# Decode bits on ScalarE, part of x on TensorE, and whole output rows in a fused attention and mixture-of-experts kernel

## The chip, the cores and the metric

The kernel runs on 1 core of one Trainium2 chip. A core has TensorE (matmuls and the loads of their weights, PE and PEld in the tables), VectorE (DVE), ScalarE (ACT), GpSimd (POOL), SyncE (SP, which here issues the DMAs), and 16 DMA engines. Each engine works through its own list of instructions in order. The metric is device time in microseconds. The kernel before takes 516.57 us, the median of 3 runs (515.62 to 517.06).

## The reference, cut to what matters

Three layers follow each other on 3072 tokens. In the first, a recurrence with decay is written here as one step per token; the kernel does it in blocks of 128 tokens.

```python
def _attn_ref(r, k, v, w, u):             # (4, 8, 768, 48) each, fp32
    state = np.zeros((B, H, D, D)); y = np.zeros_like(r)
    for t in range(S):
        cur = np.einsum('bhd,bhe->bhde', u[None] * kt, vt)
        y[:, :, t] = np.einsum('bhd,bhde->bhe', rt, state + cur)
        state = wt[:, :, :, None] * state + np.einsum('bhd,bhe->bhde', kt, vt)
    return y

def _moe_ref(x, w_in, w_out):             # x (3072, 384); weights Float64
    h = x @ w_in                          # (3072, 2048)
    return ((h * np.cos(h)) @ w_out).astype(np.float32)

def _moe2_ref(x, phi, w1, w2):            # soft routing over 32 slots, 8 experts
    logits = x @ phi
    d = softmax over tokens of logits;  slot_input = d.T @ x
    slot_out[e] = np.maximum(slot_input[e] @ w1[e], 0.0) @ w2[e]
    c = softmax over slots of logits
    return c @ slot_out                   # (3072, 384) fp32
```

## The kernel before

**Tiling.** The 3072 tokens are 24 blocks j of 128. For each block the attention part makes transposes, two scans (L150, L158), small matmuls (A, U, y) and at last `x`, the block's output with channels on the partitions. x is kept as two parts, a rounded one and a remainder. ScalarE copies the high part out of PSUM with rounding (`xh`, L289), VectorE subtracts it from the PSUM tile to get the low part (`xl`, L293). The matmuls of the second layer (`h`, L413 to L415) take three products of such parts: nine matmuls of 512 columns for one bank, four banks per block. Each bank passes through `turns` (ScalarE, L428), `rest` (VectorE, L432), `cos` (ScalarE, L436), `mul` (VectorE, L440) and transposes (`gT`, L447), and is reduced to slot logits (`l`, L462) and slot sums (`E`, L558).

**Decoding the weights.** `w_in` and `w_out` come as Float64. They are read as pairs of 32-bit words in 16 pieces of 768 numbers per partition, eight of each matrix (`raw`, L308 and L314), and turned into fp32 by bit operations, four steps a piece. `abs` on ScalarE (L319) takes the high word, scaled so that its bits stand nearly in place; `d1` on VectorE (L323) shifts them left by three; `d2a` on VectorE (L328) puts the sign in; `d2b` on VectorE (L334) shifts the low word right by 29 and sets these three bits. A piece of `w_in` is then also split: `whi` (ScalarE, L344) rounds it, `wn` on TensorE (L355, L356) makes the piece minus its rounded part by two products with the identity and with `neg`, its negative, and `wc` (ScalarE, L361) copies the remainder. Pieces of `w_out` are transposed (L367), copied (L373) and multiplied with `phi`.

**Order.** All this is one long table of steps, HEAD. Its order is the order of the instructions on every engine; nothing is reordered afterwards. A step's name and numbers call one of the functions below: `d1.i.3` is `e_shift("i", 3)`, `xl.0` is `e_xl(0)`. The first DMAs are the constants `cs` (L599), then pieces 0 and 1 of `w_in`.

**End.** After the 24 blocks come the 8 experts (L746, L786) and the output. The output is c @ slot_out for 24 tiles of 128 tokens. Its 384 columns are made in two parts, 256 and 128 wide, since the second part of `slot_out` (`so`, and rounded as `sr`) is ready later. `outputs(i, n0)` makes part i for two or four tiles at a time: matmuls (L817 for the first four tiles, L819 for the others), one copy of the PSUM bank by ScalarE or VectorE (L826), one DMA (L827). Its rows are 1 KB long in part 0 and 512 bytes in part 1.

Of the kernel before, what the change touches and what calls it, by code (L numbers as in the profile page):

```python
# [21 lines left out]
def rwkv_moe_kernel(ctx: ExitStack, tc: tile.TileContext, r, k, v, w, u, w_in, w_out, phi, w1, w2, cst, out):  # L22
# [21 lines left out]
    JA = 6  # L44
    ATT = 77
# [22 lines left out]
    dec = d_stack.enter_context(tc.tile_pool(name="dec", bufs=4))  # L68
# [230 lines left out]

    def e_raw(x, n):  # L300

        if x == "i":
# [295 lines left out]
    if True:  # L598
        nc.sync.dma_start(cs, cst)  # L599
# [3 lines left out]
        nc.scalar.mul(neg, ident, -1.0)  # L603
# [43 lines left out]
        def exp_table():  # L647
            nc.scalar.activation(half_pi[:, 1:2], half_pi[:, 0:1], AF.Exp)

        step = {"tab": exp_table, "quart": lambda g: s_quarters(g, lcp[g]), "esl": lambda g, hf: s_e(g, slice(hf * 256, hf * 256 + 256)),  # L650
                "misc": misc, "raw": e_raw, "abs": e_abs, "d1": e_shift, "d2a": e_sign, "d2b": e_d2b, "whi": e_whi, "wlo": e_wlo, "oT": e_oT, "oc": e_oc, "om": e_om,
# [56 lines left out]
        with tc.manual_schedule(engines=ORDERED):  # L708
# [92 lines left out]
            obs = {}  # L801

            def outputs(i, n0, tile_=None):
# [23 lines left out]
                nc.sync.dma_start(out[(n0 * nt + t0) * 128:(n0 * nt + t1) * 128, cols].rearrange("(t p) f -> p t f", p=128), ob)  # L827

# [167 lines left out]
```

## Time and profile before

| | |
|---|---|
| median of 3 runs | 516.57 us (515.62 to 517.06) |
| the profiled execution | 517.23 us |
| its span in the trace | 515.5 us |
| busy in the span | TensorE 475.0, VectorE 426.2, ScalarE 318.6, GpSimd 103.1 us |
| the chain that ended last, by engine | TensorE 70%, VectorE 20%, ScalarE 4%, issue 3% |
| mean granted clock of TensorE | 0.986 of 2.4 GHz |

The span is what the trace covers, from the first to the last event; 1.73 us of the execution lie outside it. Busy time of TensorE is modelled, since its matmuls are pipelined. Which engine limits the kernel differs from stage to stage, so the table's shares are averages over stages; a view of busy time in separate stretches tells more.

### The profile page before, as it was taken

How to read it: one execution, taken by the hardware profiler on the slowest of the kernel's cores; microseconds unless marked ns; L12 is line 12 of the kernel's file. 1: busy time of each engine (PE TensorE's matmuls, PEld its weight loads, DVE VectorE, ACT ScalarE, POOL GpSimd, SP SyncE). 2: the span in 40 equal slices, each digit the busy share in tenths (PEclk: the TensorE clock that was granted, in tenths of full speed). 3: DMA queues.
4: the chain of work that ended last, by engine and by line, in shares of the span. 5: the costliest groups of instructions: out<-in, count | busy, mean ns of one | idle time of the engine just before them, and what ended most of it. 6: DMA issues, size and time to landing. Idle time of an engine off the chain costs nothing.

```text
span 515.5 us, 15594 instructions
## 1 busy us (share of the span) xinstructions
PE 475.0 (92%) x6515; PEld 369.7 (72%) x6515; DVE 426.2 (83%) x842; ACT 318.6 (62%) x702; POOL 103.1 (20%) x127
## 2 busy tenths in 40 slices
PE   1778899999999999999999999999999989997994
PEld 1545578887877787778878778778787777864573
DVE  2999999999997989979998899998898975664423
ACT  3476678776576566666756767757566655573421
POOL 2133231122423221132212312241211000002200
PEclk9979999999999999999999999999999999999997
DMA  9998384932540930505532208224311964089948
GB/s 263 268 267 152 117 207 112 173 70 53 94 78 3 145 57 3 93 3 82 91 62 40 42 17 136 50 49 80 65 19 28 409 263 156 17 309 355 399 142 269
DMA packets 144758, 67.47 MB, mean 131 GB/s; under 512 B 127153, under 2 KB 133553, under 8 KB 144689
## 3 DMA queue, kind: packets, MB, share of 16 engines
q1 hardware_dynamic: 144688, 66.49, 51.2%
q8 instruction: 51, 0.84, 0.7%
q14 instruction: 19, 0.15, 0.1%
HBM read 61.75 MB, written 4.72 MB: 129 GB/s over the span
## 4 chain that ended last, share of the span: by engine, by line
PE 70%; DVE 20%; ACT 4%; issue 3%; DMA 1%; SPq 0%; DVEq 0%; ACTq 0%
PE h L413 11%; PE h L415 10%; PE h L414 10%; PE gT L447 7%; PE l L462 4%; PE y L275 4%; PE E L558 3%; PE A L196 2%; PE hps L746 2%; PE so L786 2%; DVE lt L179 2%; PE U L247 2%; DVE pt L158 2%; PE kT L135 2%; DVE qt L150 2%
## 5 line engine op out<-in xcount | busy, mean ns | idle before, releaser
L413 PE MATMUL h<-wu,x 128*128 128x512 f32 x288 | 119.3, 414 | 1.1 <-DVE g L440 0.6
L415 PE MATMUL h<-wu,x 128*128 128x512 f32 x288 | 113.0, 392 | 0.0
L414 PE MATMUL h<-wu,x 128*128 128x512 f32 x288 | 112.4, 390 | 0.0
L436 ACT ACTIVATE g<-g,half_pi 128x512 f32<-128x512 f32 x97 | 69.0, 718 | 28.5 <-DVE g L432 27.6
L428 ACT ACTIVATE g<-h 128x512 int32<-128x512 f32 (+1 forms) x96 | 57.1, 597 | 47.5 <-PE h L415 43.5
L440 DVE TENSOR_TENSOR g<-g,h 128x512 f32<-128x512 f32 x96 | 64.9, 677 | 12.4 <-ACT g L436 11.4
L432 DVE SCALAR_TENSOR_TENSOR g<-g,h 128x512 f32<-128x512 int32 (+1 forms) x96 | 64.5, 677 | 10.8 <-ACT g L428 9.7
L210 POOL TENSOR_SCALAR_AFFINE_SELECT lt<-bo 64x512 f32<-64x512 f32 x48 | 38.1, 794 | 173.8 <-ACT bo L238 89.5
L413 PEld LDWEIGHTS h<-wu,x 128*128 128x128 f32 x288 | 54.2, 188 | 15.6 <-DVE g L440 4.3
L453 ACT COPY gt<-gT 128x512 f32<-128x512 f32 x89 | 51.8, 583 | 19.9 <-PE gT L447 15.1
L415 PEld LDWEIGHTS h<-wu,x 128*128 128x128 f32 x288 | 54.0, 188 | 12.0
L414 PEld LDWEIGHTS h<-wu,x 128*128 128x128 f32 x288 | 54.3, 189 | 9.2
L447 PE MATMUL gT<-cs,g 128*128 128x128 f32 x384 | 58.6, 278 | 0.8 <-DVE g L440 0.5
L447 PEld LDWEIGHTS gT<-cs,g 128*128 128x128 f32 x384 | 43.5, 141 | 11.9 <-issue 2.0
L163 POOL TENSOR_TENSOR ru<-rn,u_b 128x384 f32<-128x384 f32 x24 | 27.7, 1154 | 116.7 <-DVE bo L233 57.5
L222 DVE COPY_PREDICATED lt<-cs,A 64x256 f32<-64x256 uint32 x72 | 32.2, 447 | 3.0 <-PE A L196 1.4
L261 ACT COPY rzs<-z 64x192 f32<-64x192 f32 x96 | 33.4, 348 | 2.0 <-DVE z L256 1.0
L179 DVE TENSOR_TENSOR lt<-rT,pt 64x512 f32<-64x512 f32 x48 | 32.8, 684 | 0.8 <-PE y L275 0.3
L462 PE MATMUL l<-gt,p_sb 128*32 128x128 f32 x768 | 32.1, 277 | 0.3 <-DVE gt L453 0.3
L158 DVE TENSOR_TENSOR_SCAN pt<-wf,ini_f 128x520 f32<-128x520 f32 x24 | 30.7, 1278 | 0.2
L150 DVE TENSOR_TENSOR_SCAN qt<-wf,one_b 128x520 f32<-128x520 f32 x24 | 29.7, 1236 | 0.1
L275 PE MATMUL y<-lt,rzs 128*32 128x64 f32 x1536 | 26.6, 220 | 3.2 <-issue 3.2
(165 smaller groups left out, 769.0 us busy)
## 6 DMA issues: line engine op xcount, KB each, us to landing
we<-in_moe_w_dram SPq DMA_DIRECT2D x16, 1536.0 KB, 9.3
rawo<-in_moe_w_out_dram SPq DMA_DIRECT2D x8, 768.0 KB, 5.1
wn<-in_w_dram SPq DMA_DIRECT2D x24, 192.0 KB, 4.1
kn<-in_k_dram SPq DMA_DIRECT2D x24, 192.0 KB, 4.4
rawi<-in_moe_w_in_dram SPq DMA_DIRECT2D x3, 1536.0 KB, 10.2
rn<-in_r_dram SPq DMA_DIRECT2D x24, 192.0 KB, 3.4
vn<-in_v_dram SPq DMA_DIRECT2D x24, 192.0 KB, 3.7
rzs<-in_v_dram SPq DMA_DIRECT2D x96, 48.0 KB, 3.0
```

Of the source, the lines that this page charges most:

```text
L179: nc.vector.tensor_tensor(out=L[h, a], in0=ps[h], in1=segs(pt, 0, C)[h], op=ALU.mult)
L275: nc.tensor.matmul(ps[m:m + 32, o, c * C:(c + 1) * C], lhsT=rz[:, c, p, a, 32 * b:32 * b + 32], rhs=L[:, a, 2 * p + c, :], start=m not in ...
L413: nc.tensor.matmul(half[:, f], lhsT=xh[:, c, :], rhs=wh, start=(c == 0), stop=False)
L414: nc.tensor.matmul(half[:, f], lhsT=xl[:, c, :], rhs=wh, start=False, stop=False)
L415: nc.tensor.matmul(half[:, f], lhsT=xh[:, c, :], rhs=wl, start=False, stop=(c == KD - 1))
L428: nc.scalar.activation(gt.bitcast(I32), hp, AF.Copy, bias=0.25, scale=1.0 / TWO_PI)
L432: nc.vector.scalar_tensor_tensor(out=gt, in0=gt.bitcast(I32), scalar=-TWO_PI, in1=hp, op0=ALU.mult, op1=ALU.add)
L436: nc.scalar.activation(gt, gt, AF.Sin, bias=half_pi[:, 0:1])
L440: nc.vector.tensor_tensor(out=gt, in0=gt, in1=hp, op=ALU.mult)
L447: nc.tensor.transpose(ps[:, m * 128:(m + 1) * 128], gt[:, m * 128:(m + 1) * 128], ident)
L453: (nc.vector.tensor_copy if n >= ATT and n % 8 in (1, 2, 5) else nc.scalar.copy)(gt_t[t, q], pend.pop(("gT", t, q)))
L462: nc.tensor.matmul(lps_t[g][32 * m:32 * m + 32, o:o + TB], lhsT=p_sb[:, 4 * q + m, :], rhs=gt[:, m * 128:(m + 1) * 128], start=first, stop ...
```

## The change

Four things change, and the whole table HEAD is written in another order.

1. **Decode.** A step `q` (`e_low`) on ScalarE takes the low word, as an unsigned integer, to the three bits that it gives: it scales by about 2^-29, adds a bias and writes an integer. `d2a` now puts the sign into that integer tile, and `d2b` shifts the high part by three and joins the two in one VectorE instruction. `d1` is gone. All 16 pieces are in the set LOW. A piece of `w_out` is decoded in place in `wo_sb`, so the pool `dec` holds two tiles of each kind instead of four.
2. **Low part of x.** For blocks 0 to 5 `xl` is replaced by `xm` on TensorE, which adds the negative of the high part to the PSUM tile, and `xc` on ScalarE, which copies the tile out with rounding. Blocks 6 to 23 keep `xl`.
3. **Start.** Piece 1 of `w_in` is the first DMA, ahead of `cs` and piece 0. Pieces 2 and 3 come as two DMAs, not one.
4. **Output.** Tiles 0 to 9 are made as before. Tiles 10 to 23 are made by `rows(k)` when both parts of `sr` are there: two matmuls of 384 columns, whose weights are every other token of 256, two copies, one by each engine, and one DMA in which every partition holds two whole rows, 3072 bytes.

```diff
-    dec = d_stack.enter_context(tc.tile_pool(name="dec", bufs=4))
+    dec = d_stack.enter_context(tc.tile_pool(name="dec", bufs=2))
...
-    neg = sm_p.tile([128, G], F32R, tag="lg", name="neg", bufs=1)[:, 0:128]
+    neg = nat.tile([128, 128], F32R, name="neg")
...
+    def e_xm(j):
+        nc.tensor.matmul(pend["xT", j], lhsT=neg, rhs=xo(j)[0], start=False, stop=True, skip_group_check=True)
+
+    def e_xc(j):
+        nc.scalar.copy(xo(j)[1], pend.pop(("xT", j)))
...
     def e_abs(x, n):
-        a_t[x, n] = dec.tile([128, 768], F32, tag="a", name=f"a{x}{n}")
+        a_t[x, n] = dec.tile([128, 768], F32, tag="a", name=f"a{x}{n}") if x == "i" else wo_sb[:, 2 * n:2 * n + 2, :].rearrange("p m n -> p (m n)")
...
+    def e_low(x, n):
+        q_i[x, n] = dec.tile([128, 768], I32, tag="q", name=f"q{x}{n}", bufs=2)
+        nc.scalar.activation(q_i[x, n].rearrange("p (k f) -> p k f", k=KD), raw_t[x, n][..., 0].bitcast(U32), AF.Copy,
+                             bias=7.5 * 2.0 ** -17 - 0.5, scale=2.0 ** -29 * (1.0 - 2.0 ** -17))
...
-        hi, ai = raw_t[x, n][..., 1], a_t[x, n].bitcast(I32).rearrange("p (k f) -> p k f", k=KD)
+        hi, ai = raw_t[x, n][..., 1], (q_i[x, n] if (x, n) in LOW else a_t[x, n].bitcast(I32)).rearrange("p (k f) -> p k f", k=KD)
...
+        if (x, n) in LOW:
+            nc.vector.scalar_tensor_tensor(out=ai, in0=ai, scalar=3, in1=q_i[x, n], op0=ALU.logical_shift_left, op1=ALU.bitwise_or)
+            return
...
-        nc.sync.dma_start(cs, cst)
...
+            NA = 10
...
+            crf = cr.rearrange("p j b t -> p (j b t)")
+
+            def rows(k):
+
+                m = k - NA // 2
+                if m in (0, 4):
+                    obs["r"] = wu_p.tile([128, 4, 2, DM], F32, tag=f"wu{1 if m == 0 else 2}", name=f"obr{m}")
+                ob = obs["r"][:, m % 4]
+                for i in range(2):
+                    ps = pb(f"r{k}_{i}")[:, 0:DM]
+                    nc.tensor.matmul(ps, lhsT=crf[:, 256 * k + i:256 * k + 256:2], rhs=sr, start=True, stop=True)
+                    (nc.vector.tensor_copy if i else nc.scalar.copy)(ob[:, i], ps)
+                nc.sync.dma_start(out[256 * k:256 * k + 256, :].rearrange("(p i) f -> p (i f)", i=2), ob.rearrange("p i f -> p (i f)"))
...
             nc.vector.tensor_copy(so[:, parts[1]], ops[1][:, 0:128])
-            for n0 in range(9, 12):
-                outputs(0, n0)
+            outputs(1, 0)
             slots_out(1)
             slots_round(1)
-            for n0 in range(6):
+            for n0 in range(1, (NA + 3) // 4):
                 outputs(1, n0)
+            for k in range(NA // 2, NTT // 2):
+                rows(k)
...
-raw.i.0 raw.i.1 lw.0 abs.i.0 d1.i.0 d2a.i.0 d2b.i.0 abs.i.1 lk.0 d1.i.1 d2a.i.1 raw.i.2 wT.0 z.0.0 lr.0 lw.1 misc d2b.i.1 kT.0 wf.0 whi.1 wn.1.1 whi.0
+raw.i.1 q.i.1 cs raw.i.0 lw.0 abs.i.1 q.i.0 z.0.0 d2a.i.1 lk.0 neg wT.0 d2b.i.1 lw.1 abs.i.0 d2a.i.0 kT.0 whi.1 wf.0 misc wn.1.0 wT.1 d2b.i.0 scan.0
```

What stands on an engine before and after is shown at three places. In these rows a tile's number is a counter and has no meaning of its own. The first is VectorE where the pieces 4 and 5 of `w_in` are decoded; before, `ai` is the tile of a piece and `rawi` the words it came in:

```order
L323 TENSOR_SCALAR ai_351<-ai_351 128x768
L328 SCALAR_TENSOR_TENSOR ai_333<-rawi_271,ai_333 128x768
L328 SCALAR_TENSOR_TENSOR ai_351<-rawi_271,ai_351 128x768
L334 SCALAR_TENSOR_TENSOR ai_333<-rawi_271,ai_333 128x768
L334 SCALAR_TENSOR_TENSOR ai_351<-rawi_271,ai_351 128x768
L323 TENSOR_SCALAR ai_358<-ai_358 128x768
L150 SCALAR_TENSOR_TENSOR qt_445<-wf,one_b 128x520
```

After the change, on the same engine, with `qi` the tile that ScalarE now writes:

```order
L343 SCALAR_TENSOR_TENSOR qi_354<-rawi_248,qi_354 128x768
L343 SCALAR_TENSOR_TENSOR qi_361<-rawi_248,qi_361 128x768
L348 SCALAR_TENSOR_TENSOR ai_352<-ai_352,qi_354 128x768
L348 SCALAR_TENSOR_TENSOR ai_412<-ai_412,qi_361 128x768
L151 SCALAR_TENSOR_TENSOR qt_438<-wf,one_b 128x520
```

The shifts of L323 are gone, two instructions a piece are left, and the scan for block 2 follows at once. The second place is TensorE behind the product y of block 0; before:

```order
L275 MATMUL y_390<-lt_125,rzs_127 32x64 x32
L196 MATMUL A_425<-lt_126,ks_324 64x64 x16
L355 MATMUL wl_0_468<-ai_333,cs 128x512
L356 MATMUL wl_0_468<-wu_447,neg 128x512
L135 MATMUL kT_471<-cs,kn_119 128x128 x4
```

After the change, where `x_114` is the high part of x that ScalarE has just written from the same PSUM tile:

```order
L276 MATMUL y_376<-lt_125,rzs_127 32x64 x32
L204 MATMUL kN_415<-cs,ks_333 128x128 x4
L136 MATMUL wT_420<-cs,wn_121 128x128 x4
L298 MATMUL y_376<-x_114,neg 128x384
L197 MATMUL A_440<-lt_126,ks_333 64x64 x16
```

Two transposes stand between y and the new matmul, which reads what ScalarE makes of y; A of block 1 is queued behind it. The third place is TensorE at the output, where the last matmuls of the experts (`so`) make the second part of slot_out; before:

```order
L786 MATMUL so_7048<-we_6942,wo_sb 32x128 x8
L819 MATMUL o_9_0_7240<-sr,cr 128x256 x2
L819 MATMUL o_10_0_7245<-sr,cr 128x256 x2
L819 MATMUL o_11_0_7250<-sr,cr 128x256 x2
L793 MATMUL sp_7255<-wo_sb,cs 96x128
L817 MATMUL o_0_0_7259<-wo_sb 128x128 x4
L819 MATMUL o_1_0_7267<-sr,cr 128x128 x4
```

After the change, with `r` for the banks of `rows`:

```order
L801 MATMUL so_7063<-we_6957,wo_sb 32x128 x8
L827 MATMUL o_0_0_7234<-wo_sb 128x128 x4
L808 MATMUL sp_7242<-wo_sb,cs 96x128
L829 MATMUL o_1_0_7246<-sr,cr 128x128 x4
L829 MATMUL o_2_0_7253<-sr,cr 128x128 x2
L862 MATMUL r_0_7259<-sr,cr 128x384
L862 MATMUL r_1_7262<-sr,cr 128x384
```

Of part 0 nothing is left to do here, and behind the two short groups of part 1 come 14 matmuls of 384 columns.

## Rows read from the trace of the kernel before

**Rows 1.** Busy time by stretch (first line: the columns).
```profile
core 0: us, PE busy (x) PEld busy (x) DVE busy (x) ACT busy (x) POOL busy (x), PEclk, DMA share, GB/s
10.00:67.00 57.00, 44.32 (x525) 31.23 (x529) 56.12 (x84) 34.87 (x69) 14.41 (x14) 0.94 0.89 214
67.00:110.00 43.00, 43.00 (x662) 35.73 (x652) 41.84 (x68) 33.41 (x73) 8.46 (x8) 1.00 0.66 144
110.00:400.00 290.00, 286.34 (x4057) 227.77 (x4051) 263.63 (x544) 191.75 (x434) 70.21 (x74) 1.00 0.34 59
```

**Rows 2.** Waits of TensorE, then of VectorE, 10 to 67: us, times, longest.
```profile
PE wl L355 <- DVE ai L334: 2.8, 1, 2.8
PE wl L355 <- DVE x L293: 2.2, 1, 2.2
...
DVE ai L323 <- ACT ai L319: 9.8, 2, 9.6
```

**Rows 3.** Line L323 alone (d1): VectorE busy by stretch.
```profile
10.00:67.00 57.00, 7.04 (x11) 0.94 0.89 214
```

**Rows 4.** Line L293 alone (xl): VectorE busy by stretch.
```profile
10.00:67.00 57.00, 1.05 (x2) 0.94 0.89 214
```

**Rows 5.** Groups of one shape: count, us, mean ns, idle before.
```profile
L323 DVE TENSOR_SCALAR ai<-ai 128x768 int32<-128x768 int32 x8 | 5.1, 643 | 9.8 <-ACT ai L319 9.8
L293 DVE TENSOR_TENSOR x<-y,x 128x384 fp32r<-128x384 f32 x24 | 13.1, 548 | 3.0 <-ACT x L289 2.9
L319 ACT ACTIVATE ai<-rawi 128x768 f32<-128x768 f32 x8 | 7.1, 904 | 6.0 <-DMA rawi<-in_moe_w_in_dram 5.1 <-PE wl L355 0.8
L289 ACT CAST x<-y 128x384 fp32r<-128x384 f32 x24 | 11.5, 480 | 6.5 <-PE y L275 6.5
```

**Rows 6.** Waits of ScalarE, 10 to 67: us, times, longest.
```profile
ACT wu L344 <- DVE ai L334: 9.0, 3, 4.3
ACT wu L361 <- PE wl L356: 3.9, 4, 1.5
ACT ksn L226 <- PE kN L203: 2.0, 1, 2.0
ACT ao L319 <- DVE wo_sb L334: 2.0, 1, 2.0
```

**Rows 7.** TensorE in order of time: start us, us.
```profile
48.43 0.39 PE L414 MATMUL h<-wu,x 128*128 128x512 f32 x1
48.66 0.39 PE L415 MATMUL h<-wu,x 128*128 128x512 f32 x1
...
51.01 0.80 PE L356 MATMUL wl<-wu,neg 128*128 128x512 f32 x1
51.65 1.12 PE L367 MATMUL woT<-cs,wo_sb 128*128 128x128 f32 x6
```

**Rows 8.** The longest waits of TensorE, 67 to 464.
```profile
PE y L275 <- issue: 3.2, 2, 2.1
```

**Rows 9.** ScalarE's first decode: start, us, idle before.
```profile
8.68 1.69 ACT L319 ACTIVATE ai<-rawi 128x768 f32<-128x768 f32 x2 [5.12 <-DMA rawi<-in_moe_w_in_dram]
```

**Rows 10.** Busy time by stretch at the output, columns as in rows 1.
```profile
475.00:480.00 5.00, 5.00 (x82) 3.37 (x80) 1.91 (x6) 1.72 (x5) 1.70 (x1) 1.00 1.04 410
505.00:508.00 3.00, 2.88 (x24) 2.54 (x23) 1.84 (x4) 1.59 (x3) 0.00 (x0) 1.00 1.04 341
508.00:514.00 6.00, 0.00 (x0) 0.00 (x0) 0.69 (x1) 0.16 (x1) 0.00 (x0) 0.53 1.03 289
```

**Rows 11.** TensorE at the output in order of time: start us, us.
```profile
500.30 1.22 PE L819 MATMUL o<-sr,cr 96*128 96x256 f32 x8
...
504.15 0.38 PE L793 MATMUL sp<-wo_sb,cs 128*96 128x128 f32 x2
504.37 1.05 PE L817 MATMUL o<-wo_sb 128*128 128x128 f32 x8
505.54 2.45 PE L819 MATMUL o<-sr,cr 96*128 96x128 f32 x20
```

More of the change, by code (lines that the diff above doesn't have):

```diff
@@ L44, in rwkv_moe_kernel @@
     JA = 6
+    NSPLIT = 4
     ATT = 77
@@ L861 @@
-wn.1.0 wc.1.1 lr.1 lv.0 scan.0 abs.i.3 wc.1.0 ks.0 kN.0 sr.0 rT.0 sp.0 d1.i.3 abs.i.2 ru.0 ksn.0 d2a.i.3 d1.i.2 wT.1 lw.2 lk.1 wf.1 wn.0.0 wc.0.0
-wn.0.1 L.0 scan.1 wc.0.1 U.0 d2b.i.3 d2a.i.2 raw.i.4 raw.i.6 st.0.0 d2b.i.2 bo.0 lr.2 z.0.1 whi.2 A.0 bs.0 sr.1 lz.0 st.0.1 rT.1 sp.1 whi.3 kT.1
-raw.o.0 ks.1 D.0 L.1 wn.3.1 abs.i.4 ru.1 kN.1 lk.2 rz.0.1 mask.0 d1.i.4 ksn.1 abs.i.5 wn.3.0 rz.0.0 abs.i.7 wn.2.0 wc.3.1 z.1.0 wc.3.0 lv.1 bo.1
-raw.o.1 wc.2.0 wT.2 d1.i.5 wn.2.1 wf.2 d2a.i.4 d2a.i.5 lw.3 lv.2 d2b.i.4 rz.1.0 y.0 d2b.i.5 d1.i.7 A.1 xh.0 bs.1 scan.2 whi.4 abs.o.0 D.1 wc.2.1
@@ L865 @@
-d2a.i.7 xl.0 whi.5 sr.2 ru.2 lz.1 lw.4 mask.1 wn.4.0 kT.2 wn.4.1 h.0.0 wc.4.0 abs.i.6 d1.o.0 ks.2 d2a.o.0 d2b.i.7 d2b.o.0 wc.4.1 abs.o.1 U.1 wT.3
-d1.i.6 turns.0.0 st.1.0 sp.2 wf.3 lr.3 z.1.1 lk.3 rest.0.0 h.0.1 rT.2 st.1.1 d1.o.1 kN.2 turns.0.1 L.2 cos.0.0 lz.2 scan.3 ksn.2 bo.2 wn.5.0 rz.1.1
-rest.0.1 lv.3 wc.5.0 z.2.0 oT.0 oc.0 oT.1 sr.3 y.1 xh.1 wn.5.1 raw.o.2 oc.1 xl.1 d2a.i.6 U.2 st.2.0 mul.0.0 lw.5 wc.5.1 wT.4 z.2.1 gT.0.0 cos.0.1
-abs.o.2 d2b.i.6 whi.6 sp.3 rT.3 d2a.o.1 h.1.0 st.2.1 wf.4 A.2 whi.7 bs.2 d2b.o.1 L.3 rz.2.0 D.2 rz.2.1 mask.2 raw.o.3 wn.6.0 wc.6.0 turns.1.0 wn.6.1
@@ new lines @@
+lr.0 whi.0 rz.0.0 ks.0 sr.0 kN.0 sp.0 raw.i.3 wc.1.0 ksn.0 rT.0 wf.1 raw.i.2 ru.0 q.i.3 wn.1.1 lv.0 lk.1 abs.i.3 L.0 wn.0.1 wn.0.0 wc.0.1 lr.1 raw.i.4
+scan.1 A.0 d2a.i.3 wc.1.1 wc.0.0 q.i.2 d2b.i.3 bo.0 lz.0 d2a.i.2 U.0 bs.0 st.0.0 kT.1 z.0.1 lw.2 lv.1 raw.o.0 D.0 raw.i.6 sr.1 abs.i.2 st.0.1 lk.2
+ru.1 whi.3 lr.2 d2b.i.2 rz.0.1 lw.3 ks.1 mask.0 wn.3.0 bo.1 sp.1 whi.2 wn.3.1 wc.3.0 wc.3.1 bs.1 abs.i.5 q.i.5 D.1 wn.2.1 q.i.4 rT.1 wn.2.0 L.1 wc.2.1
+z.1.0 y.0 d2a.i.5 d2a.i.4 wc.2.0 abs.i.4 xh.0 kN.1 wT.2 ksn.1 d2b.i.5 wf.2 xm.0 d2b.i.4 raw.o.1 whi.5 xc.0 q.o.0 scan.2 A.1 U.1 whi.4 abs.o.0 mask.1
@@ new lines @@
+rz.1.0 q.i.7 h.0.0 st.1.0 d2a.o.0 turns.0.0 z.1.1 d2b.o.0 st.1.1 wn.4.0 wc.4.0 ru.2 sr.2 lv.2 wn.4.1 abs.i.7 z.2.0 kT.2 rz.1.1 lz.1 wc.4.1 sp.2
+rest.0.0 d2a.i.7 raw.o.2 cos.0.0 ks.2 oT.0 lr.3 oc.0 d2b.i.7 h.0.1 wT.3 rT.2 q.i.6 wn.5.0 wf.3 L.2 q.o.1 lw.4 wc.5.0 kN.2 scan.3 lv.3 wn.5.1 y.1
+d2a.i.6 ksn.2 mul.0.0 wc.5.1 lk.3 abs.i.6 U.2 st.2.0 lz.2 bo.2 d2b.i.6 xh.1 z.2.1 whi.7 d2a.o.1 sr.3 st.2.1 xm.1 gT.0.0 xc.1 abs.o.1 oT.1 oc.1 raw.o.3
+whi.6 q.o.2 turns.0.1 sp.3 h.1.0 wn.6.1 wT.4 wc.6.1 d2b.o.1 rest.0.1 rT.3 L.3 rz.2.0 wn.6.0 bs.2 wf.4 turns.1.0 D.2 A.2 wc.6.0 cos.0.1 wn.7.0 ru.3
@@ new lines @@
+gc.0.0 rz.2.1 kT.3 wc.7.0 mask.2 lk.4 mul.0.1 y.2 abs.o.2 rest.1.0 h.0.2 oT.3 cos.1.0 q.o.3 ks.3 xh.2 oT.2 d2a.o.2 bo.3 xm.2 z.3.0 abs.o.3 oc.3 scan.4
+gT.0.1 oc.2 xc.2 lr.4 turns.0.2 bs.3 wn.7.1 d2b.o.2 lz.3 d2a.o.3 wc.7.1 mul.1.0 D.3 kN.3 A.3 gc.0.1 rest.0.2 raw.o.4 mask.3 cos.0.2 mul.0.2 kT.4 h.1.1
+d2b.o.3 sr.4 ks.4 ksn.3 lk.5 sp.4 abs.o.4 q.o.4 oT.4 oT.5 turns.1.1 h.0.3 raw.o.5 lv.4 gT.0.2 oc.4 rz.3.0 oc.5 oT.7 rest.1.1 q.o.5 U.3 d2a.o.4 st.3.0
+om.0 oc.7 gc.0.2 oT.6 lw.5 z.3.1 kN.4 st.3.1 turns.0.3 pc.0 ru.4 oc.6 wT.5 pT.0 cos.1.1 om.1 z.4.0 ps.0 rest.0.3 ksn.4 d2a.o.5 lv.5 raw.o.7 mul.1.1
```

221 lines of the change are left out of this document (112 added, 109 removed).

## The prediction

> **What bounds the kernel now.** I read the busy time by stretch first, then the waits of each engine in the stretch where no engine is obviously the last, then single lines, and the end in order of time. In the stretches the reader is to see two regimes [rows 1]. From 10 to 67 us VectorE is busy 56.12 of 57 us and TensorE only 44.32, so TensorE stands idle 12.7 us there. From 67 to 110 TensorE is busy 43.00 of 43, and from 110 to 400 it is busy 286.34 of 290. The waits of TensorE in the first regime were ended by VectorE: the longest by the decode of a weight piece (2.8 us) and by xl (2.2), while VectorE itself waited once, 9.6 us at the very start, for the first piece [rows 2]. So VectorE sets the pace of the ramp up to 67 us, and TensorE that of everything to the output. A microsecond taken from VectorE before 67 moves all of the rest forward; one taken after 67 frees an engine that TensorE doesn't wait for. At the output TensorE ends at about 508, and from 505 to 514 the DMA engines are full, at 341 and then 289 GB/s [rows 10]: there the DMAs are last.
>
> **The change part by part.** *VectorE in the ramp.* Of the 16 shifts d1, 11 run between 10 and 67, 7.04 us together [rows 3], and 5 later; of the six removed xl, 2 run there, 1.05 us [rows 4]. d2a and d2b stay, with the same number of elements and the same kind of instruction, and I leave them at their length. That is 8.1 us of VectorE. In a packed stream an instruction begins before its neighbour has ended: two abs of 904 ns [rows 5] took 1.69 us in a row [rows 9], 7% less than their sum. These here are shorter, and I take off a tenth: 7.2 us. From below: d1 has a mean of 643 ns and xl, of half the elements, 548 [rows 5]; if the long ones among d1 only hand their delay to a neighbour, 13 times 0.48 is 6.2 us. I take -7.2, between -8.1 and -6.2. What goes behind 67 counts nothing, since TensorE's own work covers them [rows 1]; should the ramp end earlier, that cover begins earlier too.
>
> *ScalarE in the ramp.* For 11 pieces it gets a step q. The trace has no such step, but it has the neighbour abs with the same 768 elements and the same spacing in memory: 904 ns [rows 5]. An integer conversion could cost less or more; with 0.6 to 1.3 us each, 11 of them are 6.6 to 14.3 us, and I take 0.90, 9.9 us. Two copies xc at xh's 480 ns are 1.0 us [rows 5]. ScalarE's 34.87 us [rows 1] become 45.8. The ramp shrinks from 57 to 49.8, so 4.0 us are left idle. Of its waits before, those ended by VectorE (9.0 and 2.0 us) go with VectorE's relief, but 3.9 and 2.0 us were ended by TensorE [rows 6] and have no reason to go: 5.9 us where 4.0 are left, an overrun of 1.9. I add +2.0, between 0 (the new order fills the waits) and +4.6 (several steps queue behind a late one).
>
> Here a rule speaks against the edit. The trace says that a shift on VectorE takes 643 ns and its successor on ScalarE some 904 [rows 5]. The Trainium skill, "ScalarE: Activation LUTs", section "Rules for kernel authors", says to put adds and multiplies on VectorE and keep ScalarE for transcendentals, since VectorE is the faster per element. By that rule alone the decode gets 16 x 0.26 = 4.2 us longer in engine time and the edit loses; by the rows it wins, since it is VectorE that the others wait for. What the rule is right about, that ScalarE pays more, is a rival below.
>
> *TensorE.* Six xm of 384 columns are new. A product with `neg` over 512 columns stood from 51.01 to the next start at 51.65, 0.64 us with the wait for its operand, and a product of 512 columns in a full stream takes 0.23 [rows 7]. So 384 columns cost 0.17 to 0.48 us each, 1.0 to 2.9 us together. Behind xm.0 stand A and U of block 1 and the first bank h, and they wait if ScalarE is late with xh. I take 0.24 each. Two or so hide in the idle time of the ramp, four stand in the full stretch: +1.0.
>
> *Start.* ScalarE's first decode began at 8.68, after a wait for the DMA of piece 0 [rows 9]. Now piece 1 goes first, and 0.16 MB of constants and piece 0 follow; at the 214 GB/s of the ramp [rows 1] the constants are 0.8 us. From below nothing, if the two pieces share the engines anyway. I take -0.6. `neg` and the transposes need the constants later than that, and wait for nothing more.
>
> *The order.* HEAD is new from end to end, and so are the waits behind 67. Before, they were small there: the longest were two of 3.2 us together that no engine ended [rows 8], in the stretch where TensorE had 3.7 of 290 us idle [rows 1]. I take 0, with -2 to +3. Two DMAs for pieces 2 and 3 add one issue on SP in front of 1.5 MB that are wanted later: nothing.
>
> *Output.* Before, TensorE reached the second part at 504.15 and its first rounded use at 505.54 [rows 11]. Eight matmuls of part 0, 1.22 us [rows 11], leave the place ahead of it, while four tiles of part 1 (1.05 us [rows 11]) come to stand before `sp`; the six matmuls of part 0 that stood in that place had been overlapped with the copy of `so`. The net is some -0.5, so `sr` is ready at about 505.0. Then 0.66 MB of 512-byte rows (10 tiles x 128 x 128 x 4) and 2.75 MB of whole rows (14 x 128 x 384 x 4) are to go out, where 1.57 MB were before. The short rows at 289 GB/s take 2.3 us, from 504.6 to about 507.0. For rows of 3072 bytes no write stands in the trace. The nearest are writes of 1 KB mostly (341 GB/s), of 512 bytes (289), and reads of the expert weights, in rows of 3072 bytes too (410) [rows 10]. 2.75 MB are 8.1, 9.5 or 6.7 us by these. From the two writes, on 16 engines, 1 KB takes 48.0 ns and 512 bytes 28.3, so 19.7 ns per 512 bytes and 8.6 fixed; 3072 bytes then 127 ns, an estimate of 388 GB/s, or 7.1 us: the end is at 514.1, where it was 514.0. So the longer rows pay back what the later start costs: 0, between -0.4 (at 410) and +2.4 (at 289). The Trainium skill, "DMA: Bandwidth & Descriptors", section "Where 436 GB/s comes from", puts a core's share of HBM at about 358 GB/s. By it the rows would take 7.7 us and the tail lose 0.6; the trace's 410 GB/s of reads goes over that limit, so I don't hold it for the writes.
>
> *Sum.* -7.2 + 2.0 + 1.0 - 0.6 + 0 + 0 = -4.8 us. Against the profiled execution's 517.23 that is 512.4; the median of the runs, 516.57, is 0.7 lower than this one execution, so I forecast 511.8.
>
> **Rivals.** *The relief passes whole.* ScalarE fills its waits, xm hides, and a ramp less bound by VectorE leaves a better place for TensorE's work: -7.2 - 0.8 + 0.5 - 1.5 = -9.0, 507.6. For it speaks that TensorE has 12.7 us idle to win back [rows 1]; against it that ScalarE would have to run at over 90%.
>
> *ScalarE becomes the bound of the ramp.* This is the rule above as a mechanism: q takes 1.1 us or its queue delays `wf`, `ksn` and `whi`, on which scans and matmuls wait. Then the ramp gives back 4.6 us, and all six xm count (1.4): -7.2 + 4.6 + 1.4 = -1.2, 515.4, no change to be measured. For it: 45.8 us of work in 49.8. Against it: VectorE ran at 98% in the same stretch and the order held.
>
> *TensorE waits for ScalarE at xm: slower.* xm stands in TensorE's queue behind y, and in between come the end of y, xh (480 ns, [rows 5]) and what ScalarE still has ahead of it, one or two steps of 0.9. If each of the six waits 1.5 us, they cost 6 x (0.24 + 1.5) = 10.4 in place of 1.0, and the sum is +4.6: 521. It decides from about 0.9 us a wait (no gain), and from 1.2 it is measurably slower. Against it: before 67 TensorE has idle time to lose, and in the table two transposes or more stand between y and xm.
>
> *The tail does not do what it should.* Whole rows go out no faster than 512-byte rows: +2.4, 514.2, faster still.
>
> **How the numbers follow.** A measurement of this kernel can tell 0.3%, 1.55 us: faster is below 515.0, slower above 518.1. The forecast has 0.48, its own range being 509.5 to 514.0; the whole relief 0.20; the weak tail 0.08, of it 0.06 faster and 0.02 within 0.3%; ScalarE as bound 0.15, of it 0.05 faster, 0.09 within and 0.01 slower; the waits at xm 0.09, of it 0.02 within and 0.07 slower. Faster: 0.48 + 0.20 + 0.06 + 0.05 = 0.79; within: 0.02 + 0.09 + 0.02 = 0.13; slower: 0.01 + 0.07 = 0.08. The range goes from 506.3, somewhat below the whole relief, to 516.8, above ScalarE as bound.
>
> **What would show it.** VectorE's busy time falls by some 12 us, ScalarE's rises by 17 (16 q near 0.9, 6 xc near 0.48). TensorE becomes full near 62 instead of 67, and its waits in the ramp are ended by ScalarE more often. The xm are 0.2 to 0.5 us long and wait less than 0.5. Between 110 and 400 TensorE is idle as little as before. At the output the DMAs move over 370 GB/s while whole rows go out and end within 0.5 us of where they did, counted from `so`. The forecast is wrong if TensorE is full no earlier than at 65, if a wait behind 67 grows to several microseconds, or if the whole rows run below 341 GB/s.

## The result, and the profile after

The changed kernel takes 508.74 us (median of 4 runs, 506.99 to 509.25) against 516.82 (4 runs) for the kernel before on the same chip: ratio 0.984, 95% interval 0.981 to 0.987, or 8.1 us less. Forecast were 511.8, in a range of 506.3 to 516.8. The profiled span is 507.0 us, where it was 515.5.

The busy time by stretch after the change, columns as in [rows 1] (PE, PEld, DVE, ACT, POOL busy, then PEclk, DMA share, GB/s):

```profile
10.00:67.00 57.00, 50.95 (x602) 37.41 (x601) 54.01 (x78) 49.19 (x95) 17.98 (x18) 0.97 1.01 239
67.00:110.00 43.00, 43.00 (x647) 36.52 (x645) 40.68 (x69) 37.01 (x86) 13.33 (x13) 1.00 0.60 125
110.00:400.00 290.00, 285.04 (x4090) 227.16 (x4093) 265.90 (x539) 189.80 (x429) 59.78 (x66) 1.00 0.37 68
```

TensorE is busy 50.95 of the 57 us from 10 to 67, 6.6 more than before [rows 1]; ScalarE went from 34.87 to 49.19. VectorE is still busy 54.01 of 57. It has less to do per piece, and the new order fills the time with later work. From 67 to 110 TensorE is as full as it was, from 110 to 400 it is idle 1.3 us more.

Waits between 10 and 67 us, the two longest of TensorE, the longest of VectorE, and of ScalarE the one that was its longest before (us, times, longest), the answer to [rows 2, 6]:

```profile
PE kT L136 <- DVE st_state L265: 2.1, 2, 2.0
PE y L276 <- issue: 1.5, 1, 1.5
...
DVE lt L180 <- PE rT L136: 1.1, 1, 1.1
...
ACT wu L361 <- DVE ai L348: 1.1, 1, 1.1
```

TensorE's waits for a decoded piece (2.8) and for xl (2.2) are gone, and ScalarE's wait for the last decode step fell from 9.0 to 1.1 us [rows 6]. In the new order q of one piece stands where ScalarE waited for another; that this is why both went is read from the order and not tested alone.

The start, ScalarE and VectorE in order of time (start us, us, idle before in brackets), the answer to [rows 9]; the last line is VectorE's first scan before the change:

```profile
5.53 0.89 ACT L333 ACTIVATE qi<-rawi 128x768 int32<-128x768 uint32 x1 [3.24 <-DMA rawi<-in_moe_w_in_dram]
...
8.14 0.90 ACT L333 ACTIVATE qi<-rawi 128x768 int32<-128x768 uint32 x1 [0.94 <-DMA rawi<-in_moe_w_in_dram]
...
11.54 1.24 DVE L151 TENSOR_TENSOR_SCAN qt<-wf,one_b 128x520 f32<-128x520 f32 x1 [0.45 <-ACT wf L146]
```

```profile
14.55 1.23 DVE L150 TENSOR_TENSOR_SCAN qt<-wf,one_b 128x520 f32<-128x520 f32 x1
```

The first decode begins 3.15 us earlier than in [rows 9], and the first scan at 11.54; before it stood at 14.55. The second piece is waited for until 8.14, about when both pieces were decoded before (8.68): one piece now comes ahead of the other.

The new and the neighbouring groups (count, busy us, mean ns, idle before), beside [rows 5]:

```profile
L333 ACT ACTIVATE qi<-rawi 128x768 int32<-128x768 uint32 x8 | 7.1, 902 | 4.2 <-DMA rawi<-in_moe_w_in_dram 4.2
L301 ACT CAST x<-y 128x384 fp32r<-128x384 f32 x6 | 2.9, 487 | 0.0
```

At the output, by stretch (columns as above), the answer to [rows 10], and the second copy of `so`, the rounding of part 1 and the issues of the whole rows in order of time:

```profile
492.00:494.00 2.00, 1.50 (x18) 1.16 (x10) 0.29 (x1) 0.13 (x1) 0.00 (x0) 1.00 0.70 235
494.00:496.00 2.00, 1.06 (x9) 1.01 (x9) 0.60 (x2) 0.70 (x3) 0.00 (x0) 1.00 0.29 85
496.00:498.00 2.00, 2.00 (x13) 2.00 (x12) 2.00 (x5) 2.00 (x6) 0.00 (x0) 1.00 0.50 142
...
500.00:502.00 2.00, 0.00 (x0) 0.00 (x0) 0.00 (x0) 0.00 (x0) 0.00 (x0) 0.56 1.03 398
502.00:504.00 2.00, 0.00 (x0) 0.00 (x0) 0.00 (x0) 0.00 (x0) 0.00 (x0) 0.50 1.03 399
```

```profile
492.26 0.29 DVE L888 COPY wo_sb<-so 128x128 f32<-128x128 f32 x1 [1.79 <-PE so L801]
...
494.65 0.29 DVE L814 TENSOR_TENSOR sr<-sp,sr 32x128 fp32r<-32x128 f32 x1 [2.09 <-ACT sr L813]
...
497.43 5.70 SPq L864 DMA_DIRECT2D out_dram<-obr  x7
```

The whole rows move at 398 GB/s, but the DMAs were busy only 29 and 50% of the time from 494 to 498: the first whole row is issued 5.2 us behind the copy of `so`.

A ledger by three marks that both traces have (us): the start of the last group's logits, the start of the first copy of `so`, and the end of the span.

| | before | after | difference |
|---|---|---|---|
| last `lc` on TensorE | 464.02 | 454.10 | -9.9 |
| from there to the first copy of `so` | 31.33 | 30.68 | -0.65 |
| from there to the end | 20.15 | 22.22 | +2.1 |

So 10.6 us were won ahead of the output, and 2.1 given back in it. The lines for the first two marks, before and after, and TensorE's stretch up to the first of them (columns as above):

```profile
464.02 0.70 PE L475 MATMUL lc<-lg,cs 128*128 128x256 f32 x2 [0.55 <-DVE lg L469]
495.35 0.37 ACT L833 COPY wo_sb<-so 128x256 f32<-128x256 f32 x1 [5.74 <-PE so L786]
...
454.10 0.70 PE L492 MATMUL lc<-lg,cs 128*128 128x256 f32 x2 [0.55 <-DVE lg L486]
484.78 0.37 ACT L870 COPY wo_sb<-so 128x256 f32<-128x256 f32 x1 [5.74 <-PE so L801]
```

```profile
400.00:464.02 64.02, 60.81 (x662) 47.04 (x660) 44.81 (x100) 39.13 (x79) 0.00 (x0) 1.00 0.61 230
...
400.00:454.10 54.10, 52.93 (x550) 40.89 (x543) 37.22 (x82) 32.60 (x66) 0.00 (x0) 1.00 0.60 225
```

Of the 9.9 us, 7.9 are idle time of TensorE: 6.6 less from 10 to 67, 2.0 less from 400 to the mark, 0.5 less before 10, and 1.3 more from 110 to 400. The other 2.1 are busy time, though six xm were added; TensorE's granted clock from 10 to 67 us rose from 0.94 to 0.97. The clock is not what makes the gain: at a mean granted clock of 0.990 over the whole span the changed kernel took 508.8 and 509.25 us, and the kernel before 516.18 to 518.05 (three of its runs beside experiments 9 to 12).

### The profile page after: what moved, and what is told of

Same layout as the page of the kernel before. It is cut to its first block, busy times and chain, and to the rows that moved or that the text cites. A ratio compares the mean times of both kernels' runs of the same rounds, so it can differ in the third digit from the quotient of the medians.

```text
span 507.0 us, 15580 instructions
## 1 busy us (share of the span) xinstructions
PE 472.6 (93%) x6507; PEld 369.4 (73%) x6507; DVE 420.1 (83%) x821; ACT 330.3 (65%) x727; POOL 101.1 (20%) x127
## 4 chain that ended last, share of the span: by engine, by line
PE 64%; DVE 25%; ACT 5%; issue 3%; DMA 1%; SPq 0%; DVEq 0%; ACTq 0%
PE h L430 9%; PE h L432 9%; PE h L431 8%; PE gT L464 6%; PE y L276 4%; PE l L479 4%; DVE lt L223 3%; DVE g L449 3%; DVE g L457 3%; PE E L575 3%; DVE pt L159 2%; PE hps L761 2%; PE so L801 2%; PE A L197 2%; DVE qt L151 2%
## 5 line engine op out<-in xcount | busy, mean ns | idle before, releaser
L430 PE MATMUL h<-wu,x 128*128 128x512 f32 (+1 forms) x288 | 118.4, 411 | 1.3 <-DVE g L457 1.0
L432 PE MATMUL h<-wu,x 128*128 128x512 f32 (+1 forms) x288 | 112.7, 391 | 0.0
L431 PE MATMUL h<-wu,x 128*128 128x512 f32 (+1 forms) x288 | 112.5, 390 | 0.0
L445 ACT ACTIVATE g<-h 128x512 int32<-128x512 f32 x96 | 56.9, 595 | 45.5 <-PE h L432 40.7
L211 POOL TENSOR_SCALAR_AFFINE_SELECT lt<-bo 64x512 f32<-64x512 f32 x48 | 36.5, 761 | 143.0 <-ACT bo L239 71.4
L164 POOL TENSOR_TENSOR ru<-rn,u_b 128x384 f32<-128x384 f32 x24 | 26.6, 1110 | 145.3 <-DMA rn<-in_r_dram 50.4
L151 DVE TENSOR_TENSOR_SCAN qt<-wf,one_b 128x520 f32<-128x520 f32 x24 | 31.2, 1300 | 0.6 <-ACT wf L146 0.5
L165 POOL TENSOR_TENSOR ru<-ru,kn 128x384 f32<-128x384 f32 x24 | 28.1, 1169 | 3.1 <-PE y L276 1.3
```

The lines of the kernel that those rows point to most:

```text
L151: nc.vector.tensor_tensor_scan(qt[:, n:0:-1], wf[:, n:0:-1], one_b[:, n:0:-1], 0.0, ALU.mult, ALU.add)
L430: nc.tensor.matmul(half[:, f], lhsT=xh[:, c, :], rhs=wh, start=(c == 0), stop=False)
L431: nc.tensor.matmul(half[:, f], lhsT=xl[:, c, :], rhs=wh, start=False, stop=False)
L432: nc.tensor.matmul(half[:, f], lhsT=xh[:, c, :], rhs=wl, start=False, stop=(c == KD - 1))
L445: nc.scalar.activation(gt.bitcast(I32), hp, AF.Copy, bias=0.25, scale=1.0 / TWO_PI)
```

## The experiments

Each ratio is to the kernel before on the same chip. Three chips were used, on which the kernel before took 517.8 to 518.1 us, so the ratios are set side by side. A hundredth in the ratio is 5.2 us.

**1. The old output stage in the changed kernel.** The edit puts the block from `obs = {}` to the end of the stage back; its last lines:

```diff
...
-            outputs(1, 0)
+            for n0 in range(9, 12):
+                outputs(0, n0)
             slots_out(1)
             slots_round(1)
-            for n0 in range(1, (NA + 3) // 4):
+            for n0 in range(6):
                 outputs(1, n0)
-            for k in range(NA // 2, NTT // 2):
-                rows(k)
```

> The changed kernel with the output stage of the kernel before (24 tiles in 512 and 1024-byte rows). Theory: the gain is made ahead of the output, and the new tail gives back some 2 us, since it takes 14.7 us from the second copy of so to the end where 12.0 stood before; with the old stage 506.7 us, the time from that copy to the end near 12. Rival: the whole rows at 398 GB/s save time, and the longer tail only follows from the earlier copy of so; then 509 us or more.

Measured: 506.67 us, ratio 0.9783 (0.9761 to 0.9805). From the first copy of `so` to the end 20.4 us stand in its profile, where the kernel before has 20.15. The theory holds: the new output stage costs 2 to 3 us (ratio 0.9823 and 0.9842 for the changed kernel).

**2. The first three loads in the old order.**

```diff
-raw.i.1 q.i.1 cs raw.i.0 lw.0 ...
+cs raw.i.0 raw.i.1 q.i.1 lw.0 ...
```

> The changed kernel with the first three loads in the order of before: constants, piece 0, piece 1; nothing else is moved. Theory: the start gained 3 us on ScalarE (first decode at 5.5 in place of 8.7) and most of that reaches the end: 511 to 512 us. Rival A, the prediction's own term: 0.6 us, 509.3. Rival B: TensorE waits for another load to 9.4 us in both kernels, so the earlier decode is worth nothing: 508.7.

Measured: 509.90 us, ratio 0.9847 (0.9825 to 0.9869), against 0.9842 and 0.9823 (experiment 6) for the changed kernel: 0.3 to 1.2 us, within the intervals. ScalarE still decodes piece 1 first, which now comes last. The first decode did go back to 8.64 us, and the first bank h began at 37.52 in place of 35.19, but most of these 2.3 us were made good by the end. Rival A's size fits, B isn't excluded, and the theory (3 us reach the end) falls.

**3. The low part of x from VectorE for all blocks** (`xm` left out, `xl` in the place of `xc`).

> The changed kernel with the low part of x of all blocks from VectorE again: no xm, no xc, xl in the place of xc. Theory: one or two of the six stand in the ramp, where VectorE gets 0.5 to 1.0 us more, and TensorE loses six products of some 0.24 us, 1.4 us in all: 507.8 to 508.7 us, no difference that can be told. Rival: without the edit the banks h wait for VectorE, 510 us or more.

Measured: 512.95 us, ratio 0.9902 (0.988 to 0.9925), 3.1 to 4.1 us above the changed kernel. The theory falls, the rival holds. A wait of TensorE (8 to 460 us) that the changed kernel doesn't have stands in this profile:

```profile
PE h L431 <- DVE x L294: 2.3, 1, 2.3
```

Where it stands, TensorE and VectorE in order of time:

```profile
53.40 0.50 PE L431 MATMUL h<-wu,x 128*128 128x512 f32 x1 [2.32 <-DVE x L294]
...
51.59 0.95 DVE L343 SCALAR_TENSOR_TENSOR qo<-rawo,qo 128x768 int32<-128x768 int32 x1
...
52.80 0.55 DVE L294 TENSOR_TENSOR x<-y,x 128x384 fp32r<-128x384 f32 x1
```

The first bank h does not wait: it begins at 35.40, 0.2 us later than in the changed kernel. It is the first bank of block 1 that waits for `xl.1`, which stands on VectorE behind two steps of the decode.

**4. The old decode in the new order** (`d1` back, no `q`; `d1 d2a` where the later of `abs` and `d2a` stood). The pool of two tiles and the decoding of `w_out` in place stay as in the changed kernel.

> The changed kernel with the decode of before (16 shifts d1 on VectorE, no q on ScalarE), d1 and d2a where the later of abs and d2a stood. Theory: VectorE bounds the ramp again and 12 d1 of 0.64 us come back in it, less the overrun of ScalarE, which goes: 514 to 516 us. Rival: the gain came from the new order and the start, and the time stays below 511 us.

Measured: 528.26 us, ratio 1.0204 (1.018 to 1.0228): 19 us above the changed kernel and 12 above the upper end of what the theory expected. The theory and its rival both fall: it is slower than the kernel before by 10.5 us, with the same decode. What of this the shifts themselves cost, and what the order with `d2a` moved, experiment 10 takes apart.

**5. The kernel before without its 16 shifts.** The edit takes `d1` out of the order.

> The kernel before with its 16 shifts d1 left out and nothing in their place (the weights are then decoded wrongly): the relief of VectorE alone, with the old order, the old start and the old output. Theory: VectorE sets the pace of the ramp, and 11 shifts of 0.64 us less are 6 to 8 us less at the end: 509 to 511 us. Rival: the old order does not let it pass, other waits take its place, and less than 3 us are gained: 514 us or more.

Measured: 515.16 us, ratio 0.9942 (0.9917 to 0.9967), 3.0 us less (1.7 to 4.3 by the interval). The theory falls, and the rival's 514 us or more holds. Its profile, the stretch of [rows 1], and below it waits of VectorE and ScalarE (us, times, longest):

```profile
10.00:67.00 57.00, 47.09 (x542) 33.25 (x543) 52.23 (x78) 37.97 (x74) 13.08 (x14) 0.94 0.92 218
```

```profile
DVE lt L179 <- PE rT L135: 1.5, 2, 1.0
...
ACT wu L344 <- DVE ai L334: 5.2, 2, 3.3
```

VectorE's busy time over the whole span fell from 426.2 to 417.0 us, 9.2 for 16 shifts. A third of that reached the end (a fifth to a half by the interval). VectorE now waits itself (4.8 us of the 57 idle, 0.9 before) for steps of the two others, and ScalarE still waits 5.2 us for decoded pieces.

**6. The changed kernel again**, as a measure for 7 and 8.

> The changed kernel once more, as a measure for the others on the same chip. Theory: its ratio to the kernel before is 0.984 again. The order of work up to the last logits is that of the run with the old output stage, in which they came at 453.1 us; they came at 454.1 in the first profile, so a spread of 1 us.

Measured: 508.74 us, ratio 0.9823 (0.9798 to 0.9849). Its last `lc` came at 455.33, in experiment 1 at 453.06: the spread of one order of work is over 2 us between executions, so a difference is taken below from the ratios and not from two profiles.

**7 and 8. `sp` first and the whole rows ahead of the short tiles; the same with 16 tiles by parts.** The edit of both; experiment 8 also sets `NA = 16` and puts the tiles of part 0 into two buffers:

```diff
-            outputs(1, 0)
             slots_out(1)
             slots_round(1)
-            for n0 in range(1, (NA + 3) // 4):
-                outputs(1, n0)
             for k in range(NA // 2, NTT // 2):
                 rows(k)
+            for n0 in range((NA + 3) // 4):
+                outputs(1, n0)
```

> The changed kernel with sp and its rounding ahead of the tiles of part 1, and the whole rows ahead of the short tiles. Theory: the DMAs stand half idle from 490 to 498 us, because the whole rows wait for the rounded part 1 behind one tile and its copy and their issue stands behind two more; sp 0.7 us earlier and the rows' issue 0.6 us earlier again give 1 to 2 us: a ratio 0.002 to 0.004 below that of the changed kernel. Rival: the bytes behind the second copy of so set the end (3.4 MB at nearly 400 GB/s), and the order among them is worth nothing.

> The same with 16 output tiles by parts and only 8 as whole rows. Theory: three double tiles of part 0 go out while the DMAs stand half idle, and behind the second copy of so there are 1.05 MB of short rows (3.6 us at 289 GB/s) and 1.57 MB of whole rows (4.0 us at 398), 7.6 us where 2.3 and 6.9 stood: 3 to 4 us less than the changed kernel, and 0 to 1 below the run with the old output stage. Rival: the short rows at the end cost what the whole rows save, and the time is that of the old output stage, 2 us below the changed kernel.

Measured: 507.89 us, ratio 0.9825 (0.9791 to 0.986), no difference that can be told; and 506.69 us, ratio 0.9784 (0.9757 to 0.9811). From the first copy of `so` to the end the profiles have 21.8 and 21.0 us, where the changed kernel has 22.2 and the old stage 20.4. In 7 the DMAs starve as they did, only earlier:

```profile
492.00:494.00 2.00, 1.33 (x9) 1.21 (x8) 0.84 (x3) 0.99 (x3) 0.00 (x0) 1.00 0.25 86
494.00:496.00 2.00, 2.00 (x16) 2.00 (x15) 2.00 (x6) 2.00 (x6) 0.00 (x0) 1.00 0.55 214
496.00:498.00 2.00, 1.00 (x10) 0.86 (x8) 1.48 (x3) 1.01 (x3) 0.00 (x0) 1.00 1.03 398
```

The place of the rows is worth nothing that can be told. More tiles ahead of part 1 look better by 2.1 us (8 against 7), but the two intervals overlap, so that the bytes ready before part 1 is done decide is likely and not shown. Experiment 8 ends with its own rival: no better than the old stage.

**9. The exchange alone, in the old order.** `q` stands in the place of each `d1`, with the new forms of `d2a` and `d2b`; it is written over the low words, and the pool keeps four tiles:

```diff
-... abs.i.0 d1.i.0 d2a.i.0 d2b.i.0 ...
+... abs.i.0 q.i.0 d2a.i.0 d2b.i.0 ...
```

> The kernel before with q on ScalarE in the place of each d1 and the two new forms of d2a and d2b, in the old order, with the old start, xl and output; q is written over the low words of the piece instead of into a tile of its own. Theory, after the run without d1: the exchange alone is worth 3 us at most in the old order, and q takes part of that back on ScalarE, so 514 to 518 us; the rest of the gain is the new order's. Rival: the exchange itself makes the gain that stands ahead of the output, some 10 us: 507 to 510 us.

Measured: 520.42 us, ratio 1.0046 (1.002 to 1.0071): slower than before, 2.4 us. The theory's range (514 to 518 us) is missed on the far side, and the rival falls. By stretch, and VectorE's longest waits from 8 to 67 us:

```profile
10.00:67.00 57.00, 46.11 (x534) 31.90 (x535) 48.07 (x72) 41.63 (x78) 15.08 (x14) 0.91 0.88 214
67.00:110.00 43.00, 40.78 (x572) 33.13 (x572) 36.89 (x60) 36.04 (x77) 8.17 (x8) 1.00 0.67 145
```

```profile
DVE rawi L343 <- ACT rawi L333: 14.4, 4, 8.5
DVE x L294 <- ACT x L290: 0.8, 1, 0.8
```

VectorE is busy 8.05 us less in the stretch. But it waits for q 14.4 us in all: 8.5 at the start, where it had waited 9.6 for abs [rows 2], and 5.9 later, where it had waited 0.2. abs and q of a piece now stand one behind the other on ScalarE, ahead of the first step on VectorE; q ahead of abs, or further ahead of its piece, was not tried in the old order. TensorE is idle behind 67 too, where it was full.

**10. Neither `d1` nor `q`, in the new order.**

> The changed kernel with the decode of before, but without d1 and without q (the weights are then decoded wrongly); d2a stands where the later of abs and d2a stood. VectorE has the work of the changed kernel, ScalarE 16 q of 0.9 us less. Theory, the prediction's term: q costs 2 us in the ramp, so 506 to 507.5 us. Rival: q is hidden in ScalarE's waits, 508 to 509 us. The difference to the run with d1 back is what the 16 shifts cost in this order: near 20 us if VectorE is all that counts there.

Measured: 517.12 us, ratio 0.9981 (0.9957 to 1.0005). Neither theory on q holds: with less work than the changed kernel it is 7 to 8 us slower. Its profile shows the wait that the changed kernel had lost (8 to 67 us):

```profile
ACT wu L361 <- DVE ai L351: 9.7, 4, 3.8
```

That this comes from `d2a`, which had to be put behind `abs` in an order in which it often runs ahead of it, is argued and not shown, and what q costs in the new order isn't settled by it. The last sentence of the expectation can be read, though: it differs from experiment 4 in the shifts alone, and 1.0204 - 0.9981 is 11.5 us, not near 20, for 16 shifts that VectorE's busy time counts as 7.9 (429.7 against 421.8). A part goes with TensorE's clock: the runs of experiment 4 had mean granted clocks of 0.976 to 0.980, and the three of experiment 10 at such a clock took 518.7 to 519.8 us, some 9 us less than experiment 4. Either way the whole cost of a shift reaches the end there.

**11. Each `q` twice, in the changed kernel.**

```diff
-raw.i.1 q.i.1 cs ...
+raw.i.1 q.i.1 q2.i.1 cs ...
```

> The changed kernel with each q issued twice. ScalarE is busy 49.2 of the 57 us from 10 to 67, so 7.8 us are left, and 12 more q of 0.9 are 10.8. Theory: ScalarE is close to its limit and becomes the bound: 4 to 8 us more than the changed kernel, 512.5 to 516.5 us. Rival: the waits of TensorE and VectorE in the ramp leave room for it, less than 2 us more.

Measured: 516.53 us, ratio 0.9973 (0.9956 to 0.999), 6.8 to 7.8 us above the changed kernel. The theory holds. By stretch, and VectorE's longest wait from 8 to 67 us:

```profile
10.00:67.00 57.00, 45.25 (x541) 32.68 (x540) 48.86 (x70) 52.75 (x94) 16.58 (x14) 0.97 0.92 214
```

```profile
DVE qi L347 <- ACT qi L337: 9.0, 4, 6.5
```

ScalarE at 52.75 of 57 us is then what VectorE waits for. How near the first q brought it to that isn't shown: ScalarE was at 49.19, and VectorE waited 0.6 us for q from 8 to 67 us.

**12. 20 tiles by parts (`NA = 20`), 4 as whole rows, `sp` first.**

> The changed kernel with sp first, 20 output tiles by parts, and 4 as whole rows in front of the short tiles. Theory: what is left behind the second copy of so is 1.31 MB of short rows (4.5 us at 289 GB/s) and 0.79 MB of whole rows (2.0 us at 398), 6.5 us where 7.6 stood with 16 tiles, and the DMAs are fed between 490 and 496 us: 0.5 to 1 us below the run with 16 tiles, near 506. Rival: the short rows are last whatever stands ahead of them, and the time is that with 16 tiles or above.

Measured: 506.83 us, ratio 0.9778 (0.9751 to 0.9806), 20.7 us from the first copy of `so` to the end. With experiments 1 and 8 it is one group (0.9778 to 0.9784) that can't be told apart: the best versions found, 2 to 3 us below the changed kernel, and the simplest of them is the changed kernel with the output stage of before.

## Why the prediction came out, and which of its steps did not

**The sum by experiments**, in ratios times 517 us, each difference with an uncertainty of 1 to 2 us: d1 away in the old order -3.0 (5), q put in +5.4 (9 against 5), the new order with its start and xm -13.6 (1 against 9, both with the old output), the new output +2.1 to +3.1 (6 and the first result against 1). Together -8.1 to -9.1, which is no check, since the steps are differences along one path and add up to the result by themselves. The forecast had -7.2, +2.0, +0.4 (xm +1.0, start -0.6, order 0) and 0. Direction and range came out, by luck: the terms were off by 4, 3, 14 and 2 to 3 us, and their errors offset each other to 3 or 4.

Of the -13.6, xm is 3 to 4 (3) and the start 0.3 to 1.2 (2), each taken back alone. The other 8 to 10 belong to the order together with what it needs, q in tiles of its own, the smaller pool and pieces 2 and 3 in two DMAs; no run takes these apart.

**"A microsecond taken from VectorE before 67 moves all of the rest forward" is the step that failed.** It was read from a share, 56.12 of 57 us busy [rows 1], and experiment 5 gives 3.0 us at the end for 9.2 us taken away. The decode is a chain over three engines (abs on ScalarE, three steps on VectorE, `whi` on ScalarE, products on TensorE, copies on ScalarE), and ScalarE waited 9.0 us for it in the same stretch [rows 6]. In the old order a third of the relief passed. In the order of experiments 4 and 10 a shift more or less passes whole. A full engine is the bound only as far as its next instruction has what it needs at once.

**"The order: I take 0" failed most.** The waits behind 67 were looked at, and as predicted little came of them: TensorE's idle time between 67 and the last `lc` fell by 0.7 us. The ramp was not looked at: there the order had 12.7 us of TensorE's idle time to win, and the changed kernel has 6.6 less. A diff that rewrites the whole order is not an edit of the parts plus noise; the same exchange lost 2.4 us in the old order (9) and is part of a gain in the new one.

**ScalarE.** q was put at 0.90 us and is 0.902, and xc at 0.48 and is 0.487. Its overrun was put at +2.0, no more than 4.6; in the old order it measured 5.4 (9 against 5), at or above the bound. In the new order a second q costs 6.8 to 7.8 us. The rival "ScalarE becomes the bound" thus has its size in the old order, but by a wait that it didn't name, VectorE's for q, with ScalarE busy 41.63 of 57 us; in the new order it comes true with twice the q. What was held against it, that "VectorE ran at 98% in the same stretch and the order held", was no argument: in experiment 9 VectorE is at 48.07 of 57 us because it waits. The Trainium skill's rule on it, "ScalarE: Activation LUTs", section "Rules for kernel authors", was weighed as engine time, 4.2 us. Experiment 9 is 2.4 us slower, but through the wait of VectorE for q and not through the time per element.

**xm.** The products take 426 ns each (median in the trace), and the waits on xh 0.5 us in all, as forecast. But the edit's worth is a wait of TensorE for `xl`: 2.3 us of the first bank of block 1 in experiment 3, and 2.2 us at `wn` in the old trace [rows 2], which the prediction read and gave no term of its own. It counted the edit as 1.05 us of VectorE against 1.0 of TensorE; taking it back costs 3.1 to 4.1, of which the wait shows 2.3. The rival's arithmetic was off as well: by its own terms (-7.2 + 2.0 - 0.6) no gain is left from 0.73 us a wait on, not 0.9, and it is measurably slower from 1.0, not 1.2.

**Start.** -0.6 was forecast. The first scan came 3.0 us earlier, the end 0.3 to 1.2 (2). That the size fits at the end is luck: the term was the constants' time (0.8 us), where the first piece came 3.15 us earlier, with neither the constants nor the other piece ahead of it or beside it, and most of that was lost on the way to the end.

**Output.** The rate was right, 398 GB/s against an estimate of 388, and "over 370 GB/s" came out. The other half, "end within 0.5 us counted from `so`", did not: it came 2.7 us later (14.74 us from the second copy of `so` to the end, 12.03 before). The step that failed is the time at which the rows begin: it was put at 3.5 us behind that copy, as if the short rows kept the DMAs busy until then. The rounded part was ready 2.7 us behind it in place of 1.5, since `outputs(1, 0)` has its four products and a copy ahead of `sp` and of ScalarE's rounding; two more short groups, the first row's two copies and the issue bring it to 5.2. The DMAs had nothing to do for more than half of 494 to 498: the ten tiles ahead of part 1 did not fill that time.

**The rivals.** The number was nearest to "the relief passes whole" (507.6), whose mechanism experiment 5 refutes. xm as a wait for ScalarE did not come. "The tail does not do what it should" came with about its size (+2.1 to +3.1, where +2.4 was said) and another cause: not a low rate, but no work for the DMAs.

**The signs.** TensorE is full earlier than forecast: from 50 to 60 us it is busy 9.85 of 10 (8.91 before), where "near 62" was expected. VectorE's busy time over the span was to fall by 12 us and fell by 6.1, ScalarE's was to rise by 17 and rose by 11.7:

```profile
PE 472.6 (93%) x6507; PEld 369.4 (73%) x6507; DVE 420.1 (83%) x821; ACT 330.3 (65%) x727; POOL 101.1 (20%) x127
```

The 16 q alone sum to 14.4 us by their records; the busy time counts an overlap of neighbours once, so a sum of durations overstates it, for a shift too (0.63 us by its record, 9.2 / 16 = 0.58 by experiment 5). For VectorE that is not all: the shifts (9.2, experiment 5) and the six xl (3.5, 423.6 against 420.1 in experiment 3) make up the 12 us when each goes alone. The records of VectorE's instructions sum to 462.6 us before and 452.0 after, 10.6 less; the busy time fell by only 6.1, so neighbours overlap less in the new order.

## What to carry to other kernels

A share of 98% shows that an engine is full, not that each of its microseconds is on the path: take the instruction away alone, before the order is touched, and see how much passes. Moving work to an engine with waits was worth here only what a new order made of those waits, so an exchange and its order are judged together, and one undone inside the other's order tells little. Fast transfers at the end need something to move: count the bytes that are ready before the last value is.

## What the runs showed of the hardware

Writes in rows of 3072 bytes ran at 398 and 399 GB/s in the changed kernel and at 395 to 403 in experiments 6 to 8, near the 410 of reads in [rows 10], and above the 289 to 341 of rows of 512 bytes and 1 KB there.

TensorE's granted clock differs between executions of one kernel: the twelve runs of experiment 10 have means from 0.977 to 0.993. In experiment 9's profile it fell in a stretch where it stayed at 1.00 in the profiles of all the other versions, behind some 2.4 us of idle time in three waits (columns as above, then TensorE in order of time):

```profile
466.50:475.12 8.62, 5.56 (x44) 2.01 (x44) 3.58 (x12) 2.22 (x11) 0.82 (x1) 0.80 0.81 283
```

```profile
470.36 3.53 PE L576 MATMUL E<-g,dt 128*32 128x256 f32 x32 [0.51 <-ACT dt L557]
```

The same products in the kernel before, with the same waits ahead of them:

```profile
467.87 1.93 PE L558 MATMUL E<-g,dt 128*32 128x256 f32 x32 [0.51 <-ACT dt L539]
```

That is 1.8 times, near the 2 between the clock's levels of 1.2 and 2.4 GHz. Of the twelve runs of experiment 9 the shortest (518.5 us) had a mean granted clock of 0.987, the longest (524.5 us) 0.974. Why the clock fell there and not in the other profiles stays open.
